# Cross-covariance attention then RWKV channel mix on one core: batch 0 with one kind of norm matmul, smaller last groups, and a block 0 in halves

## The chip, the cores and the metric

The kernel runs on one core of a Trainium2 chip. The metric is device time in microseconds (us). The engines have short names in the profile: PE (TensorE, matmul; PEld is its weight load), DVE (VectorE), ACT (ScalarE), POOL (GpSimd) and SP (SyncE, which only issues DMAs here).

## The reference

There are four batches of q, k and v, each 6208 x 256 in fp32. Per batch:

```python
qn = q / (np.linalg.norm(q, axis=1, keepdims=True) + 1e-06)
kn = k / (np.linalg.norm(k, axis=1, keepdims=True) + 1e-06)
s = kn.transpose(0, 2, 1) @ qn / tau
a = softmax(s)                      # over the last axis, 256 x 256
x = v @ a
# channel mix, with w_k 256x1024, w_v 1024x256, w_r 256x256
xk = mu_k * x + (1 - mu_k) * x_prev # x_prev: x one row earlier, 0 in the first row
xr = mu_r * x + (1 - mu_r) * x_prev
out = sigmoid(xr @ w_r) * (np.maximum(xk @ w_k, 0) ** 2 @ w_v)
```

The norms run over the 6208 rows, so nothing of a batch's output can begin before all of its q and k have been read.

## The kernel before, in words

**Two phases for batch 0, then one long pipeline.** q and k of batch 0 are loaded first, in fp32, by SP's queue. From its attention matrix a_sb the kernel then computes the output block by block: a block has 512 rows, there are 12 blocks per batch, 48 in all, and one block of leftover rows at the end. While the blocks run, q and k of the next batch are loaded (as bf16, by POOL's queue) and their products are slipped in between, in units of 128 rows.

**Batch 0, by groups.** `sizes` gives the groups: one of 64 rows (64 partitions, one row each), eleven of 512 rows (four rows per partition) and two of 256 rows (two per partition). `group_load` (L121) issues two DMAs, q and k, into fp32 buffers of which there are six each. `group_cast` (L138) makes a bf16 copy on DVE (L142) and squares on ACT (L144). `unit_matmul` (L171) adds k against q into S (s_ps, L182). The sums of squares come by one of two ways. Up to group `DIRECT` = 9, `group_norms` (L191) multiplies a ones matrix with the squares into the tile ssq_ps (L197), with one row in 32 lines of the array; from group 10 on, `norms_direct` (L203) uses the squares as weights and one column of ones as the moving operand, so that 128 sums land on 128 partitions of the tile `bank` (L210). Before group 10's matmuls ssq_ps is copied out by DVE (L225) and turned by four fp32 matmuls into the same `bank` (L232). `keep_warm(n)` (L509) issues n matmuls whose result is not used (junk_ps, L513); groups 5 to 9 have three each.

**From S to the first block.** `roots` takes the square root of the four columns in `bank` on ACT (L249), which needs a table load; `evac` copies S out of PSUM on ACT (L265); one activation on a tile `gate` loads the Exp table (L586). `invert` adds 1e-6 and takes the reciprocal on DVE (L257, L258) and makes two diagonal matrices rq_d (L260). `turn` (L272) multiplies S with these, which transposes and scales it into st_ps; `exp` (L280) takes exponentials and row sums on ACT; `weigh_dve` (L293, L294) divides. `v_transpose_pe` (L325) transposes a block of v on PE. `x_first` (L357) multiplies v with a_sb for block 0: one 512-column PSUM tile for each of the two d rows, the first copied out by ACT (L367), the second by DVE (L368). For later blocks `x_half` does this, one d row at a time (L352, L354).

**The pipeline.** The loop `for i in range(-2, NBLK - 1)` has eight steps j per i. Each step issues, in this order: `finish` (tanh on ACT, L469; product on DVE, L470; output DMA) of block i, one piece of a batch's softmax chain if one is due, `up(i + 1, j)` (two matmuls with w_k, L423, and a relu on ACT into kr, L428), `square` (kk = kr * kr on DVE, L441), `down(i, j - 1)` (with w_r, L456, and w_v, L460), `x_half`, `mix_delta` and `mix` of block i + 2 (DVE, L398 and L408), and in the steps named by `slots` one unit of the next batch: its two S matmuls, and ahead of it the squares of the next two rows on ACT (L163). The squares are added up on DVE by `next_add` (L169), at most once in steps 1, 6 and 7 of a block, and in step 2 at the end of a batch. The scheduling is manual: every engine runs its instructions in the order in which the program issues them. PSUM tiles rotate by tag; kT_ps, junk_ps and vT_ps share three buffers, x_first's tiles and vr_ps share two. `early` are the first four units of batch 1, whose matmuls are done at i = -1 and whose squares at i = 0. Block 1's v is transposed on PE before the loop and copied out by ACT; blocks 2 and 3 in the loop, copied out by DVE (L335); the others by a transposing DMA.

Of the kernel before, what the change touches and what calls it, by code (L numbers as in the profile page):

```python
# [10 lines left out]
F32 = mybir.dt.float32  # L11
# [7 lines left out]
def kernel(  # L19
# [44 lines left out]
    thirty2 = const.tile([P, P], F32, name="thirty2")  # L64
    nc.vector.memset(thirty2, 1.0 / 32)

# [26 lines left out]
    summed = set()  # L93
    DIRECT = NB - 3

    def sizes(b):
        return [1] + [S] * (NB - 1) + ([S // 2] * 2 if b == 0 else [S])
# [23 lines left out]
    def group_load(b, g):  # L121
# [3 lines left out]
        if b == 0:  # L125
            qk2 = pq.tile([P, S, 2, C], BF16, name="qk2", tag="qk2", bufs=4)
# [44 lines left out]
    def unit_matmul(b, g, s):  # L171
# [3 lines left out]
        if t0:  # L175

            cov[b] = (ps.tile([P, 2, C], F32, name="s_ps", tag="s_ps" if b else "vr_ps", bufs=1 if b else 2),
                      ps.tile([P, 2 * C], F32, name="ssq_ps", tag="vr_ps", bufs=2) if b == 0 else None)
        s_ps = cov[b][0] if b or g <= DIRECT else cov["s"]
# [5 lines left out]
        if s == n - 1 and b == 0:  # L185
            if g > DIRECT:
                norms_direct(g)
            else:
                group_norms(b, g)

    def group_norms(b, g):  # L191

        rows, n = rows_of(b, g)
        ssq_ps = cov[b][1]
        qk2 = groups[b, g][1]
        for u in range(n):
            nc.tensor.matmul(ssq_ps[32 * u:32 * (u + 1)], ones[:rows, :32],  # L197
                             qk2[:rows, u].rearrange("p i c -> p (i c)"),
                             start=u not in summed, stop=g == DIRECT, tile_position=(0, 32 * u),
                             skip_group_check=True)  # L200
            summed.add(u)

    def norms_direct(g):  # L203

        rows, n = rows_of(0, g)
        qk2 = groups[0, g][1]
        for u in range(n):
            flat = qk2[:rows, u].rearrange("p i c -> p (i c)")
            for i in range(4):
                nc.tensor.matmul(bank[0][:, C + i:C + i + 1], flat[:, i * P:(i + 1) * P], ones[:rows, 0:1],  # L210
                                 start=False, stop=g == len(sizes(0)) - 1 and u == n - 1, skip_group_check=True)

    def softmax_pieces(b):

        s_ps, ssq_ps = cov.pop(b) if b else cov[b]
# [7 lines left out]
        def copies():  # L223
            cov["ssq"] = pn.tile([P, 2 * C], F32, name="ssq", tag="ssq", bufs=1)
            nc.vector.tensor_copy(cov["ssq"], ssq_ps)  # L225

        def gather():

            cov["s"] = cov[b][0]
            bank[b] = ps.tile([P, 2 * C], F32, name="bank", tag="xT_ps", bufs=2)  # L230
            for i in range(4):
                nc.tensor.matmul(bank[b][:, C + i:C + i + 1], cov["ssq"][:, i * P:(i + 1) * P], thirty2[:, 0:1],  # L232
                                 start=i == 0, stop=False, skip_group_check=True)

# [5 lines left out]
        def norms():  # L240
            bank[b] = ps.tile([P, 2 * C], F32, name="bank", tag="xT_ps", bufs=2)
            for t, rows in ((sums.pop((b, "left"))[:, 0], L), (sums.pop(b), P)):
                for i in range(4):
                    nc.tensor.matmul(bank[b][:, C + i:C + i + 1], t[:rows, i * P:(i + 1) * P], ones[:rows, 0:1],
                                     start=rows == L and i == 0, stop=rows == P, skip_group_check=True)

        def roots():
            if b == 0:
                nc.scalar.activation(rn, bank[b][:, C:C + 4], AF.Sqrt)  # L249
            else:  # L250
                nc.scalar.copy(rn, bank[b][:, C:C + 4])
# [463 lines left out]
```

## Time and profile before

| | us |
|---|---|
| median of 8 runs | 514.49 |
| lowest and highest | 513.57, 515.03 |
| the profiled execution: its own time | 513.71 |
| the profiled execution: span, first to last instruction | 511.9 |
| mean granted TensorE clock | 0.996 |
| first fp32 load issued | 0.74 |
| last square of batch 0 ends (ACT, L144) | 36.74 |
| square root (ACT, L249) | 38.45 |
| first projection matmul of block 0 (PE, L423) | 45.67 |

How to read it: a line of the timeline has start, duration, engine, source line, operation, tile written from tiles read, the count of merged instructions, and in brackets the idle time before it with what ended it. A matmul's duration includes its way through the array, so matmuls overlap; the distance between two starts is what one costs. A line of the stretches has the stretch, its length, the busy time of PE, PEld, DVE, ACT and POOL (with counts), the granted clock as a share of full speed, the busy share of the DMA engines and GB/s.

### The profile page before, as it was taken

The page shows a single profiled execution, that of the slowest core. Times are in us where ns is not written, and L with a number is a line of the kernel's source. Part 1 is how long each engine was busy: PE and PEld are TensorE (multiplying, and loading weights), DVE is VectorE, ACT ScalarE, POOL GpSimd, SP SyncE. Part 2 cuts the span into 40 slices and gives each one's busy share as a digit, 9 for nine tenths or more (in the row PEclk, how much of TensorE's full clock was granted, in tenths as well). Part 3 has the DMA queues.
Part 4 walks back from the last instruction along what each step waited for, and adds up shares of the span by engine and source line. Part 5 has one row for each costly group of instructions (what it writes and reads, how often), then busy time and mean ns, then how long its engine had stood idle before and what let it go on. Part 6 is the DMA issues. An engine that isn't in the chain of part 4 may idle for free.

```text
span 511.9 us, 9496 instructions
## 1 busy us (share of the span) xinstructions
PE 494.2 (97%) x3540; PEld 336.4 (66%) x3540; DVE 439.8 (86%) x725; ACT 449.9 (88%) x924; POOL 99.8 (20%) x146
## 2 busy tenths in 40 slices
PE   3889999999999999999999999999999999999996
PEld 2454666766576667667666667667666666666675
DVE  4556899999999999999979999999878787878884
ACT  5886999999899999999899999999887888888784
POOL 0044342223054132221243133000131100000000
PEclk9989999999999999999999999999999999999999
DMA  8999999999999999998599999926496773423123
GB/s 314 410 312 198 197 167 183 140 176 199 215 177 188 174 193 161 193 193 132 99 152 208 163 198 178 182 71 119 83 181 132 123 126 90 100 81 85 44 81 103
DMA packets 133462, 83.46 MB, mean 163 GB/s; under 512 B 50660, under 2 KB 126760, under 8 KB 133416
## 3 DMA queue, kind: packets, MB, share of 16 engines
q0 software_dynamic: 56592, 33.01, 50.4%
q1 hardware_dynamic: 76656, 49.72, 43.9%
q8 instruction: 27, 0.44, 0.4%
q10 hardware_dynamic: 168, 0.13, 0.1%
q14 instruction: 19, 0.16, 0.1%
HBM read 78.71 MB, written 25.43 MB: 203 GB/s over the span
## 4 chain that ended last, share of the span: by engine, by line
PE 85%; DMA 5%; DVE 4%; ACT 4%; issue 1%; SPq 0%; DVEq 0%
PE vr_ps L460 31%; PE kT_ps L423 30%; PE vr_ps L456 8%; PE xT_ps L352 7%; PE s_ps L182 6%; DMA f<-in_k_dram 5%; ACT kr L428 1%; DVE acc L169 1%; DVE xk L408 1%; DVE kk L441 1%; PE st_ps L272 1%; ACT sq L163 1%; ACT xT L354 1%; DVE delta L398 1%; PE junk_ps L513 0%
## 5 line engine op out<-in xcount | busy, mean ns | idle before, releaser
L428 ACT ACTIVATE kr<-kT_ps 128x512 bf16<-128x512 f32 (+1 forms) x392 | 232.7, 605 | 28.9 <-PE kT_ps L423 24.9
L423 PE MATMUL kT_ps<-xk,w_k_sb 128*128 128x512 bf16 (+1 forms) x784 | 231.2, 377 | 0.4 <-DVE xk L408 0.2
L460 PE MATMUL vr_ps<-w_v_sb,kk 128*128 128x256 bf16 x1536 | 231.0, 273 | 0.1
L460 PEld LDWEIGHTS <-kk 128*128 128x128 bf16 x1536 | 149.6, 98 | 58.9 <-DVE kk L441 1.1
L470 DVE SCALAR_TENSOR_TENSOR res<-res,vr_ps 128x256 f32<-128x256 f32 x192 | 79.9, 416 | 44.1 <-ACT res L469 44.1
L441 DVE TENSOR_TENSOR kk<-kr 128x1536 bf16<-128x1536 bf16 (+2 forms) x148 | 116.9, 790 | 0.2 <-ACT kr L428 0.2
L423 PEld LDWEIGHTS <-w_k_sb 128*128 128x128 bf16 x784 | 75.8, 98 | 28.6 <-issue 1.2
L169 DVE TENSOR_TENSOR acc<-acc,sq 128x1024 f32<-128x1024 f32 x69 | 84.0, 1218 | 0.0
L182 PE MATMUL s_ps<-qk 128*128 128x256 bf16 x392 | 73.0, 287 | 5.9 <-DVE qk L142 5.9
L469 ACT ACTIVATE res<-vr_ps 128x256 f32<-128x256 f32 x192 | 76.2, 397 | 1.3 <-PE vr_ps L460 1.3
L456 PE MATMUL vr_ps<-w_r_sb,xr 128*128 128x256 bf16 x384 | 73.3, 272 | 1.2 <-DVE res L470 1.2
L408 DVE SCALAR_TENSOR_TENSOR xk<-delta,mu_t,xT 128x512 bf16<-128x512 bf16 x96 | 71.4, 745 | 0.0
L408 DVE SCALAR_TENSOR_TENSOR xr<-delta,mu_t,xT 128x512 bf16<-128x512 bf16 x96 | 71.4, 745 | 0.0
L456 PEld LDWEIGHTS <-xr 128*128 128x128 bf16 x384 | 37.6, 98 | 46.4 <-issue 2.5
L354 ACT CAST xT<-xT_ps 128x512 bf16<-128x512 f32 x94 | 55.3, 589 | 12.1 <-PE xT_ps L352 12.1
L352 PE MATMUL xT_ps<-vT,a_sb 128*128 128x512 bf16 x188 | 55.9, 379 | 0.2 <-DVE vT L335 0.2
L136 POOL DMA_DIRECT2D qk<-in_q_dram x39 | 26.3, 673 | 142.3 <-ACT kr L428 61.0
L165 ACT ACTIVATE sq<-qk 128x1024 f32<-128x1024 bf16 (+1 forms) x49 | 50.8, 1036 | 0.0
L182 PEld LDWEIGHTS <-qk 128*128 128x128 bf16 x392 | 39.1, 102 | 17.3 <-issue 7.9
L315 POOL DMA_DIRECT2D v_bf<-in_v_dram x48 | 37.3, 781 | 50.0 <-DMA vT<-v_bf 21.3
L398 DVE TENSOR_TENSOR delta<-xT 128x1024 bf16<-128x1024 bf16 x48 | 32.9, 686 | 1.9 <-ACT xT L354 1.8
L144 ACT ACTIVATE qk<-f 128x1024 bf16<-128x1024 f32 (+2 forms) x28 | 26.0, 947 | 7.9 <-DMA f<-in_q_dram 4.6
(82 smaller groups left out, 214.1 us busy)
## 6 DMA issues: line engine op xcount, KB each, us to landing
out_dram<-res SPq DMA_DIRECT2D x47, 512.0 KB, 5.0
v_bf<-in_v_dram POOLq DMA_DIRECT2D x48, 256.0 KB, 10.1
qk<-in_q_dram POOLq DMA_DIRECT2D x36, 256.0 KB, 9.2
qk<-in_k_dram POOLq DMA_DIRECT2D x36, 256.0 KB, 10.1
f<-in_q_dram SPq DMA_DIRECT2D x11, 512.0 KB, 8.7
f<-in_k_dram SPq DMA_DIRECT2D x11, 512.0 KB, 9.6
vT<-v_bf SPq DMA_TRANSPOSE x44, 9.7
f<-in_q_dram SPq DMA_DIRECT2D x2, 256.0 KB, 8.8
```

The source lines that it names most:

```text
L169: nc.vector.tensor_tensor(sums[b], sums[b], t, op=OP.add)
L182: nc.tensor.matmul(s_ps[:, ih, :], rows_at(qk, b, g, 0)[:rows, s, ih * P:(ih + 1) * P], rows_at(qk, b, g, 1)[:rows, s, :], start=t0 and ih ...
L352: nc.tensor.matmul(xT_ps, a_sb[:, b, ih, dh * P:(dh + 1) * P], vT[:, :, ih, :], start=ih == 0, stop=ih == 1)
L354: nc.scalar.copy(xT[:, dh, 1:], xT_ps)
L408: nc.vector.scalar_tensor_tensor(o[:, dh], st[i, "d"][:, dh], mu[:, dh:dh + 1], st[i, "x"][:, dh, :M], op0=OP.mult, op1=OP.add)
L423: nc.tensor.matmul(kT_ps[:, :m], w_k_sb[:, dh, fh * P:(fh + 1) * P], xk[:, dh, :m], start=dh == 0, stop=dh == 1)
L428: nc.scalar.activation(kr, kT_ps[:, :m], AF.Relu, scale=0.5 ** 0.5)
L441: nc.vector.tensor_tensor(st[i, "kk"][:, fh // 4 * 4 + lo:fh + 1, :m], kr, kr, op=OP.mult)
L456: nc.tensor.matmul(vr_ps[:, D:], xr[:, dh, s * P:(s + 1) * P], w_r_sb[:, dh, :], start=dh == 0, stop=dh == 1)
L460: nc.tensor.matmul(vr_ps[:, :D], kk[:, fh, s * P:(s + 1) * P], w_v_sb[:, fh, :], start=fh == 0, stop=fh == 7)
L469: nc.scalar.activation(res[:, s], vr_ps[:, D:], AF.Tanh, scale=0.5)
L470: nc.vector.scalar_tensor_tensor(res[:, s], res[:, s], 1.0, vr_ps[:, :D], op0=OP.add, op1=OP.mult)
```

## The change

- Batch 0's sums of squares are all made in the one-column way, into a `bank` of four columns that is opened at the start; ssq_ps, its copy and the gather are gone.
- The last 512 rows are split in groups of two, one and one rows per partition instead of two and two.
- `keep_warm` runs after every group from 5 on: three, then two, one and four matmuls.
- A first activation loads the square-root table at the start (the built program has two table loads instead of three: this one, and Exp's); the two small mu loads go from ACT's queue to POOL's.
- S is scaled by DVE while it is copied out of PSUM, and turned with the identity; ACT's copy and rq_d are gone for batch 0. The four turn matmuls run in the order of the scaled pieces.
- Block 0's v is transposed after the turn and copied out by DVE and ACT, a half each; the second half of a_sb is written in two pieces.
- Block 0 is computed in halves of 256 rows: x (both d rows of a half in one PSUM tile), the mix, and the first three of the eight `up` steps (`up_first`).
- Order: w_r and w_v are loaded ahead of block 2's v and batch 1's first group; `early` is gone, so batch 1's units begin at i = 0, j = 5, with seven per i from 1 to 6 and five at i = 7; block 1's v is transposed at (-1, 3), block 2's at (0, 3) and block 3's at (0, 6), all copied out by DVE; x, delta and xk of blocks 1 and 2 come at j = 4 to 7 instead of 0 to 5.

The marks @@ give the line before the change; `mix_tiles` only allocates delta, xk and xr.

```diff
...
-        return [1] + [S] * (NB - 1) + ([S // 2] * 2 if b == 0 else [S])
+        return [1] + [S] * (NB - 1) + ([2, 1, 1] if b == 0 else [S])
@@ L173
         if t0:
-            cov[b] = (ps.tile([P, 2, C], F32, name="s_ps", tag="s_ps" if b else "vr_ps", bufs=1 if b else 2),
-                      ps.tile([P, 2 * C], F32, name="ssq_ps", tag="vr_ps", bufs=2) if b == 0 else None)
-        s_ps = cov[b][0] if b or g <= DIRECT else cov["s"]
+            cov[b] = ps.tile([P, 2, C], F32, name="s_ps", tag="s_ps" if b else "vr_ps", bufs=1 if b else 2)
+            if b == 0:
+                bank[0] = ps.tile([P, 4], F32, name="bank", tag="xT_ps", bufs=2)
+        s_ps = cov[b]
         qk = groups[b, g][0]
...
         if s == n - 1 and b == 0:
-            if g > DIRECT:
-                norms_direct(g)
-            else:
-                group_norms(b, g)
...
+            for u in range(n):
+                flat = groups[0, g][1][:rows, u].rearrange("p i c -> p (i c)")
+                for i in range(4):
+                    nc.tensor.matmul(bank[0][:, i:i + 1], flat[:, i * P:(i + 1) * P], ones[:rows, 0:1],
+                                     start=g == 1 and u == 0 and i == 0, stop=te, skip_group_check=True)
...
-        s_ps, ssq_ps = cov.pop(b) if b else cov[b]
+        s_ps = cov.pop(b)
         rn = pn.tile([P, 4], F32, name="rn")
...
@@ L257
             for h in range(2):
-                nc.vector.tensor_scalar_mul(rq_d[:, h * P:(h + 1) * P], ident_f, rn[:, h:h + 1])
+                if b:
+                    nc.vector.tensor_scalar_mul(rq_d[:, h * P:(h + 1) * P], ident_f, rn[:, h:h + 1])
+                else:
+                    nc.vector.tensor_scalar_mul(s_sb[:, h], s_ps[:, h], rn[:, h:h + 1])
             if inv_tau != 1.0:
@@ L267
             st_ps[b] = ps.tile([P, 2, C], F32, name="st_ps", tag="xT_ps", bufs=2)
-            for ih in range(2):
-                for dh in range(2):
-                    nc.tensor.matmul(st_ps[b][:, ih, dh * P:(dh + 1) * P], s_sb[:, dh, ih * P:(ih + 1) * P],
-                                     rq_d[:, dh * P:(dh + 1) * P], start=True, stop=True)
+            for n in range(4):
+                ih, dh = (n % 2, n // 2) if b == 0 else (n // 2, n % 2)
+                nc.tensor.matmul(st_ps[b][:, ih, dh * P:(dh + 1) * P], s_sb[:, dh, ih * P:(ih + 1) * P],
+                                 rq_d[:, dh * P:(dh + 1) * P] if b else ident_f, start=True, stop=True)
@@ L288
-        def weigh_dve():
-            for ih in range(2):
-                nc.vector.reciprocal(sm[:, ih:ih + 1], sm[:, ih:ih + 1])
-                nc.vector.tensor_scalar_mul(a_sb[:, b, ih, :], e_sb[:, ih], sm[:, ih:ih + 1])
+        def weigh_dve(ih):
+            nc.vector.reciprocal(sm[:, ih:ih + 1], sm[:, ih:ih + 1])
+            for dh in (slice(0, C),) if ih == 0 else (slice(0, P), slice(P, C)):
+                nc.vector.tensor_scalar_mul(a_sb[:, b, ih, dh], e_sb[:, ih, dh], sm[:, ih:ih + 1])
         if b == 0:
-            return [copies, gather, roots, evac, invert, turn, exp, weigh_dve]
+            return [roots, invert, turn, exp, weigh_dve]
...
+        if evac is None:
+            return [lambda e=e, h=h: e(vT[:, h:h + 2], vT_ps[:, h:h + 2])
+                    for e, h in ((nc.vector.tensor_copy, 0), (nc.scalar.copy, 2))]
+        evac(vT, vT_ps)
@@ L357
         st[0, "x"] = xT
+        mix_tiles(0)
+        delta, xk = st[0, "d"], st[0, "xk"]
         nc.vector.memset(xT[:, :, 0:1], 0.0)
...
+        def go():
+            vT = st[0, "vT"]
+            x_ps = [ps.tile([P, 2, M // 2], F32, name="x_ps", tag="vr_ps", bufs=2) for a in range(2)]
+            for ih in range(2):
+                for a in range(2):
+                    for dh in range(2):
+                        nc.tensor.matmul(x_ps[a][:, dh], a_sb[:, 0, ih, dh * P:(dh + 1) * P],
+                                         vT[:, 2 * a:2 * a + 2, ih, :], start=ih == 0 and dh == 0, stop=ih == 1,
+                                         skip_group_check=True)
+            H = M // 2
+            nc.scalar.copy(xT[:, 0, 1:1 + H], x_ps[0][:, 0])
+            nc.vector.tensor_copy(xT[:, 1, 1:1 + H], x_ps[0][:, 1])
+            nc.scalar.copy(xT[:, :, 1 + H:], x_ps[1])
+            for a in range(2):
+                c = slice(a * H, (a + 1) * H)
+                nc.vector.tensor_tensor(delta[:, :, c], xT[:, :, a * H + 1:(a + 1) * H + 1], xT[:, :, c], op=OP.subtract)
+                for dh in range(2):
+                    nc.vector.scalar_tensor_tensor(xk[:, dh, c], delta[:, dh, c], mu_k_t[:, dh:dh + 1],
+                                                   xT[:, dh, c], op0=OP.mult, op1=OP.add)
+        return go
+    def up_first(fh, a):
+        H = M // 2
+        c = slice(a * H, (a + 1) * H)
+        if (fh, a) == (0, 0):
+            st[0, "kk"] = p2.tile([P, 8, M], BF16, name="kk", tag="kk", bufs=2)
+            st[0, "kr", 0] = p2.tile([P, 4, M], BF16, name="kr", tag="kr", bufs=2)
+        if a == 0:
+            st[0, "kT", fh] = ps.tile([P, M], F32, name="kT_ps", tag="kT_ps", bufs=3)
+        kT_ps = st[0, "kT", fh][:, c]
+        for dh in range(2):
+            nc.tensor.matmul(kT_ps, w_k_sb[:, dh, fh * P:(fh + 1) * P], st[0, "xk"][:, dh, c],
+                             start=dh == 0, stop=dh == 1)
+        nc.scalar.activation(st[0, "kr", 0][:, fh, c], kT_ps, AF.Relu, scale=0.5 ** 0.5)
@@ L503
-    nc.scalar.dma_start(mu_rows[0:2], moe_mu_k.rearrange("(h p) -> h p", p=P))
-    nc.scalar.dma_start(mu_rows[2:4], moe_mu_r.rearrange("(h p) -> h p", p=P))
+    nc.scalar.activation(gate, ones[:, 0:1], AF.Sqrt)
+    nc.gpsimd.dma_start(mu_rows[0:2], moe_mu_k.rearrange("(h p) -> h p", p=P))
+    nc.gpsimd.dma_start(mu_rows[2:4], moe_mu_r.rearrange("(h p) -> h p", p=P))
@@ L518
         group_cast(0, g)
-        if g == DIRECT + 1:
-            copies, gather, roots, evac, invert, turn, exp, weigh = softmax_pieces(0)
-            copies()
-            gather()
         for s in range(sizes(0)[g]):
             unit_matmul(0, g, s)
-        if 5 <= g <= DIRECT:
-            keep_warm(3)
+        if g >= 5:
+            keep_warm({S: 3, 2: 2, 1: 1}[sizes(0)[g]] if g < len(sizes(0)) - 1 else 4)
         if g == NB - 1:
@@ L575
     v_load(1)
+    nc.gpsimd.dma_start(w_r_sb, moe_w_r.rearrange("(ko ki) d -> ki ko d", ki=P))
+    nc.gpsimd.dma_start(w_v_sb, moe_w_v.rearrange("(fo fi) d -> fi fo d", fi=P))
+    v_load(2)
     next_load()
-    nc.gpsimd.dma_start(w_r_sb, moe_w_r.rearrange("(ko ki) d -> ki ko d", ki=P))
-    v_load(2)
-    nc.gpsimd.dma_start(w_v_sb, moe_w_v.rearrange("(fo fi) d -> fi fo d", fi=P))
     v_load(3)
     next_load()
+    x_go = x_first()
+    roots, invert, turn, exp, weigh = softmax_pieces(0)
     roots()
-    evac()
     nc.scalar.activation(gate, ones[:, 0:1], AF.Exp)
-    keep_warm(2)
-    go = v_transpose_pe(0, nc.vector.tensor_copy)
     invert()
-    keep_warm(2)
     turn()
-    go()
-    keep_warm(6)
+    vT_lo, vT_hi = v_transpose_pe(0, None)
     exp()
-    weigh()
-    x_first()
-    keep_warm(7)
-    v_transpose_pe(1, nc.scalar.copy)()
-    keep_warm(2)
-    early = units[:S]
-    pos["mm"] = pos["sq"] = S
+    vT_lo()
+    vT_hi()
+    weigh(0)
+    weigh(1)
+    keep_warm(3)
+    x_go()
+    keep_warm(4)
+    pos["mm"] = pos["sq"] = 0
@@ L621
                     piece()
-            if 0 <= i + 1 < NBLK:
+            if i == -1 and j < 3:
+                for fh, a in (((0, 0), (1, 0), (2, 0), (0, 1)), ((1, 1),), ((2, 1),))[j]:
+                    up_first(fh, a)
+            elif 0 <= i + 1 < NBLK:
                 up(i + 1, j)
@@ L632
                 down(i - 1, 7)
-            if i + 2 < NBLK:
+            if 0 < i + 2 < NBLK:
                 n = i + 2
-                full = 0 < n < NBLK - 1
-                if j in (0, 2) and full:
-                    x_half(n, int(j > 0))
-                if j == 3:
+                at = (4, 5, 6, 6, 7) if n < 3 else (0, 2, 3, 4, 5)
+                if n < NBLK - 1:
+                    for dh in range(2):
+                        if j == at[dh]:
+                            x_half(n, dh)
+                if j == at[2]:
                     mix_delta(n)
-                if j in (4, 5):
-                    mix(n, "xk", int(j > 4))
+                for dh in range(2):
+                    if j == at[3 + dh]:
+                        mix(n, "xk", dh)
...
                 mix(i + 1, "xr", int(j > 0))
-            if (i, j) in ((-1, 5), (0, 4)):
-                v_transpose_pe(i + 3, nc.vector.tensor_copy)()
+            if (i, j) in ((-1, 3), (0, 3), (0, 6)):
+                v_transpose_pe({(-1, 3): 1, (0, 3): 2, (0, 6): 3}[i, j], nc.vector.tensor_copy)
             if j == 5 and 4 <= i + 5 < NBLK - 1:
                 v_transpose(i + 5)
-            if i == -1 and j in (5, 6):
-                for u in early[:2] if j == 5 else early[2:]:
-                    unit_matmul(*u)
-            if (i, j) in ((0, 1), (0, 3)):
-                unit_square(*early[j - 1])
             elif i < 7:
-                slots = (1, 2, 3, 4, 5, 7) if i < 3 else (1, 2, 3, 4, 5, 6, 7)
+                slots = (1, 2, 3, 4, 5, 6, 7)
             elif i == 7:
-                slots = (1, 2, 7)
+                slots = (1, 2, 3, 4, 7)
```

## The prediction

> **What bounds the kernel now.** I read the page's first part, then the granted clock and busy times by stretch, then the timeline of the first 60 us, then TensorE's timeline alone.
>
> ```profile
> span 511.9 us, 9496 instructions
> PE 494.2 (97%) x3540; PEld 336.4 (66%) x3540; DVE 439.8 (86%) x725; ACT 449.9 (88%) x924; POOL 99.8 (20%) x146
> ```
>
> TensorE (PE) is the bound on average. Only the first 137 us can change, because the change touches batch 0, block 0 and the order of work in blocks 0 to 9. The stretches (us, busy us per engine, granted clock, DMA share, GB/s) split that part:
>
> ```profile
> 30.00:32.00 2.00, 0.71 (x3) 0.10 (x1) 1.51 (x3) 1.80 (x2) 0.00 (x0) 1.00 1.02 399
> 34.00:35.00 1.00, 1.00 (x20) 0.85 (x19) 0.83 (x3) 1.00 (x3) 1.00 (x2) 0.50 0.28 100
> 53.00:64.00 11.00, 10.88 (x80) 7.43 (x80) 9.03 (x16) 10.97 (x25) 3.26 (x6) 1.00 1.29 196
> 125.00:136.00 11.00, 9.82 (x69) 6.38 (x67) 11.00 (x17) 10.01 (x21) 0.15 (x1) 1.00 1.33 203
> ```
>
> Until 33 us the DMA is full (399 GB/s). At 34 us PE is the bound at half clock. From 53 to 64 ACT is full, at 125 DVE is full and PE waits. Next the serial path from the last load to the first projection:
>
> ```profile
> 36.76 1.28 ACT L249 ACT_TABLE_LOAD   x1
> 38.45 0.17 ACT L249 ACTIVATE rn<-bank 128x4 f32<-128x4 f32 x1 [0.41 <-PE bank L210]
> 39.76 1.13 PE L272 MATMUL st_ps<-rq_d,s_sb 128*128 128x128 f32 x8
> 43.24 0.69 DVE L368 CAST xT<-xT_ps 128x512 bf16<-128x512 f32 x1 [0.69 <-PE xT_ps L365]
> 44.77 1.42 DVE L408 SCALAR_TENSOR_TENSOR xk<-delta,mu_t,xT 128x512 bf16<-128x512 bf16 x2
> 46.24 0.38 PE L423 MATMUL kT_ps<-xk,w_k_sb 128*128 128x512 bf16 x1 [0.19 <-DVE xk L408]
> ```
>
> The square root waits for PE and not for its table, which came 0.41 us earlier. From the first kT matmul (45.67) PE's work is fixed, so the end is that start plus work plus stalls. A matmul of 512 columns takes 0.215 us from start to start (two from 47.74 to 48.17), one of 256 takes 0.109. Longer distances are stalls; the large ones are here:
>
> ```profile
> 53.12 0.59 PE L352 MATMUL xT_ps<-vT,a_sb 128*128 128x512 bf16 x2 [0.23 <-DVE vT L335]
> ...
> 131.74 0.38 PE L456 MATMUL vr_ps<-w_r_sb,xr 128*128 128x256 bf16 x2 [0.82 <-DVE res L470]
> ...
> 134.20 0.38 PE L456 MATMUL vr_ps<-w_r_sb,xr 128*128 128x256 bf16 x2 [0.35 <-DVE res L470]
> ```
>
> Start to start, from 45.67 to 140 us they are 1.4 (up to 53), 1.0 (53 to 87) and 1.8 (127 to 137), 4.2 us in all. After 140 PE hardly stops, and nothing there changes.
>
> **Loads and norms.** The ssq matmuls, their copy (0.68, L225) and the gather (0.92 of PE at 32.23) go. 16 one-column matmuls per group come: eight took 0.21 (37.43 to 37.64), so 0.42, against 0.33 for the four ssq matmuls (24.43 to 24.76): +0.1 per 2.56 us group, in PE's idle time. Casts and squares stay; the last two groups of one row give ACT four 256-column squares for two of 512 (0.31 apart by the 64x256 squares, 1.24 for 1.15), so ACT ends near 36.9 instead of 36.74. The one extra pair of DMAs moves the same bytes: nothing, up to 0.1. The mu loads go to POOL: an issue there takes 0.7 to 1.3 us (v_bf 1.34, w_k 0.74), so mu lands 2 to 4 us later and PE and DVE begin group 1 that much later; DVE needs 0.69 per cast and a cast comes every 1.28, so the lag is gone by 15 us: nothing. The first table load hides before the first load lands (4.30). On POOL's queue w_r and w_v (0.72 and 0.92 of issue) go ahead of block 2's v and of batch 1's first pair; a v load lands 10.1 us after its issue in the median, so all are there by 52, and v is first used at 56, batch 1 at 59, w_v at 53: nothing.
>
> Tail, at full clock: the last full group's k cast ends at 34.15. PE then does eight S matmuls (0.87), 16 norms (0.42), junk 3 (0.65), S 0.43, norms 0.21, junk 2 (0.43), S 0.22, norms 0.11, junk 0.21, S 0.22, norms 0.11 plus 0.15 of latency: 38.2, of which junk is 1.3. Now it is 38.41. Gain 0.2. At half clock until 37.2, as now, it would be 1.2 later.
>
> The row for the clock: after PE stood still for 1.53 us (30.71 to 32.23) and then did the slow gather, the clock is 0.50 from 33.83 for 3.41 us. [...]
>
> **From the root to the first projection.** Root 38.26 to 38.43. The Exp table (1.28) and the gate (0.21) are over at 39.9, before they are needed. DVE: add and reciprocal (0.17, 0.18) to 38.85, then S scaled in two 128x256 pieces. Nearest rows: 0.35 (a_sb, L294) and 0.42 (res, L470, out of PSUM); I take 0.37, 0.30 apart: 39.26 and 39.55. The turn needs only the first piece to begin: 39.32, four fp32 matmuls at 0.25 and latency: 40.45 (now 40.89). Exp waits for all four, as now: 40.49. V's transposes now stand behind the turn on PE (0.45), so DVE's half copy of vT (0.36) ends at 41.33 and delays the weights: second half of a_sb 42.27 (now 42.54). ACT's half copy ends 42.08. PE: eight 256-column matmuls, first half complete at 42.72.
>
> Copies: the halves put both d rows of one half in one PSUM bank, and the built program makes DVE's copy wait for ACT's. Now the two run side by side from two banks (43.03 and 43.24). The price is one ACT copy, 0.38 by the res row. [...]
>
> So ACT to 43.14, DVE to 43.55, delta half 0.37 to 43.94, xk halves 0.40 each, 0.33 apart: 44.37 and 44.70. First kT matmul 44.43 (now 45.67): **-1.24**. The second half of xk is ready at 45.43 and 45.76.
>
> **From there on.** Block 1's eight transposes move from the junk before 45.67 into PE's counted work: **+0.45**. The four early units move to the block steps i = 1, 2 and 7: no work added; batch 1's softmax pieces then come two steps later, with four steps to spare before block 12 needs them. Stalls:
> - Halves: PE waits for xk 0.22, 0.18, 0.22, and for the first kT buffer (six ACT halves, 0.26 apart) 0.13: 0.75.
> - vT of block 1 is now DVE's, behind block 0's xr: PE waits from 47.80 to 48.30: 0.5.
> - Stall c: block 1's x now comes at j = 4 and 5: x ends at 49.6, ACT's copy at 50.44, kk (0.61) and delta to 51.3, xk 52.09 and 52.76. PE is through with block 0 at 50.46, and nothing is left to do there (the early units and vT of block 2 filled it): 1.69 + 0.45. The lower bound is the present stall there, 0.7.
> - Stall d: block 2. At j = 5 the first unit puts four squares (4 x 0.52) on ACT ahead of kr 6 and tanh; DVE's res waits for the tanh, and the second xk half (0.66) is queued behind res. ACT: x copy 60.1, squares 62.1, kr, tanh 63.0, res 63.4, xk 64.1. PE is there at 62.5: 1.6. Lower bound 0, if the squares find ACT idle earlier.
> - Later: DVE gets at most three adds per block (10.05 us with 1.13 each) against PE's 10.2 with seven units. Now block 8 has four adds, which makes the 1.8 at 127 to 137. I take 0.6 for all after 64; bounds 0.2 and 1.0.
>
> Sum 5.6 against 4.2: **+1.4**. Total -1.24 + 0.45 + 1.4 = +0.6 on the profiled execution's 513.71 us (span 511.9 and 1.8 around it): **514.3 us**. The runs' median is 514.49, 0.8 above that execution; on the median the sum would be 515.1. I keep 514.3, because the half-clock stretch that the new junk covers is the one thing I see there that need not fall the same in each run; this is a choice.
>
> **Rivals.** Noise first: 0.2% (1.0 us) is about what a measurement tells from no change, so "same" is 513.46 to 515.52.
>
> Rival A, faster: the two block stalls are smaller because ACT has idle time before the squares (c 1.4, d 0.6, later 0.3, in all 3.55): -1.24 + 0.45 - 0.65 = -1.4, 512.3 us. For it: ACT is lighter than now in block 1 (six square instructions instead of nine). Against it: the order on ACT and DVE is fixed.
>
> Rival B, slower: the stall at 50.5 to 52.8 throws PE's clock. It is longer than the 1.53 us that did so at 30.71. Half clock for 3.41 us costs 1.7 of PE's work, all of it on the path: 516.0 us. [...]
>
> Rival C, the change does not do what it says: one-column matmuls do not keep the clock, the tail runs at half clock: +1.2, 515.5 us.
>
> **Chances.** Forecast 0.42, A 0.33, B 0.17, C 0.08. Faster 0.34 (A and an edge), slower 0.22 (B, half of C, an edge), same 0.44. The range goes from A's 512.2 to 516.2 just over B; the forecast's own is 513.4 to 515.5.
>
> **What would show it.** Root at about 38.3 and clock 1.00 through 34 to 38 (else C); first kT at 44.4; kT of block 1 at 52 with a PE gap of about 2 us before it, and again at 62 to 64 behind xk (no gaps: A); no gap at 130 to 135; a clock of 0.50 after 52 is B. I would be wrong most easily in the two block stalls.

## The result, and the profile after

The changed kernel takes 516.99 us in the median (516.53 to 520.23) against 514.03 for the kernel before in the same comparison: a ratio of 1.0062, 95% interval 1.0048 to 1.0075. It is slower by 3 us, and outside the predicted range. Of its twelve runs seven had a mean clock of 0.998 or more and took 516.5 to 517.3, and five, the profiled execution (518.14 us, 0.993) among them, had 0.988 to 0.995 and took 518.1 to 520.2.

The first part of the page after:

```profile
span 516.3 us, 9740 instructions
PE 494.7 (96%) x3654; PEld 340.9 (66%) x3654; DVE 440.7 (85%) x730; ACT 449.5 (87%) x929; POOL 100.9 (20%) x148
```

DVE and ACT have as much work as before; the span is longer by 4.4 us, because PE waits more and, for 3.41 us, runs at half clock. By stretch (us, busy us of PE, PEld, DVE, ACT, POOL, granted clock, DMA share, GB/s):

```profile
30.00:32.00 2.00, 1.74 (x27) 1.16 (x25) 0.99 (x2) 1.70 (x2) 0.00 (x0) 1.00 1.01 396
34.00:35.00 1.00, 0.85 (x8) 0.77 (x8) 0.79 (x3) 1.00 (x3) 1.00 (x2) 1.00 0.23 71
53.94:66.82 12.88, 11.52 (x79) 7.58 (x78) 8.08 (x14) 10.28 (x21) 1.80 (x3) 0.87 1.23 185
125.00:136.00 11.00, 11.00 (x81) 7.65 (x79) 11.00 (x18) 10.97 (x26) 2.73 (x4) 1.00 1.37 190
```

PE is busy at 30 us and the clock is 1.00 at 34, as was meant; no run tells the new junk's share in this from that of the gather, which is gone. PE's gap at 125 to 136 is gone. In its place stands block 1 (53.94 to 66.82, 12.88 us), where PE stands still and the clock is 0.87. Before, block 1 took 11.01 us:

```profile
52.93:63.94 11.01, 10.82 (x79) 7.37 (x79) 9.04 (x16) 10.98 (x24) 3.33 (x6) 1.00 1.29 196
```

The path from the root to the first projection:

```profile
38.17 0.17 ACT L211 ACTIVATE rn<-bank 128x4 f32<-128x4 f32 x1 [1.45 <-PE bank L184]
38.36 1.28 ACT L583 ACT_TABLE_LOAD   x1
38.86 0.88 DVE L225 TENSOR_SCALAR s_sb<-s_ps,rn 128x256 f32<-128x256 f32 x2
39.40 1.16 PE L237 MATMUL st_ps<-ident_f,s_sb 128*128 128x128 f32 x8 [0.39 <-DVE s_sb L225]
42.90 0.38 ACT L340 CAST xT<-x_ps 128x256 bf16<-128x256 f32 x1 [0.80 <-PE x_ps L336]
43.30 0.43 DVE L341 CAST xT<-x_ps 128x256 bf16<-128x256 f32 x1 [0.79 <-ACT xT L340]
44.23 0.88 DVE L347 SCALAR_TENSOR_TENSOR xk<-delta,mu_t,xT 128x256 bf16<-128x256 bf16 x2
44.86 0.90 PE L362 MATMUL kT_ps<-xk,w_k_sb 128*128 128x256 bf16 x5 [0.92 <-DVE xk L347]
```

The first projection starts 0.81 us earlier than before (45.67). Then PE's timeline shows where more than that is lost:

```profile
52.86 0.39 PE L422 MATMUL kT_ps<-xk,w_k_sb 128*128 128x512 bf16 x1 [1.57 <-DVE xk L407]
53.52 0.81 PE L422 MATMUL kT_ps<-xk,w_k_sb 128*128 128x512 bf16 x3 [0.27 <-DVE xk L407]
...
66.41 0.38 PE L422 MATMUL kT_ps<-xk,w_k_sb 128*128 128x512 bf16 x1 [1.36 <-DVE xk L407]
...
161.11 0.79 PE L318 MATMUL xT_ps<-vT,a_sb 128*128 128x512 bf16 x2 [0.29 <-ACT a_sb L254]
```

These are the prediction's stalls c (start to start, less the matmul: 1.73 and 0.44) and d (1.53), and one that it had ruled out: block 12's x waits for batch 1's attention matrix (0.45 and 0.18). After 170 us nothing differs.

### The profile page after: what moved, and what is told of

Same layout as the page of the kernel before. It is cut to its first block, busy times and chain, and to the rows that moved or that the text cites. A ratio compares the mean times of both kernels' runs of the same rounds, so it can differ in the third digit from the quotient of the medians.

```text
span 516.3 us, 9740 instructions
## 1 busy us (share of the span) xinstructions
PE 494.7 (96%) x3654; PEld 340.9 (66%) x3654; DVE 440.7 (85%) x730; ACT 449.5 (87%) x929; POOL 100.9 (20%) x148
## 4 chain that ended last, share of the span: by engine, by line
PE 80%; DVE 7%; DMA 6%; ACT 6%; issue 1%; SPq 1%; DVEq 0%
PE vr_ps L459 29%; PE kT_ps L422 28%; PE vr_ps L455 7%; PE xT_ps L318 7%; DMA f<-in_k_dram 6%; PE s_ps L177 5%; ACT kr L427 2%; DVE acc L164 2%; ACT sq L158 2%; DVE kk L440 1%; DVE xk L407 1%; PE st_ps L237 1%; SPq L126 1%; DVE res L469 1%; ACT xT L320 1%
## 5 line engine op out<-in xcount | busy, mean ns | idle before, releaser
L427 ACT ACTIVATE kr<-kT_ps 128x512 bf16<-128x512 f32 (+1 forms) x389 | 230.0, 603 | 30.7 <-PE kT_ps L422 26.4
L407 DVE SCALAR_TENSOR_TENSOR xk<-delta,mu_t,xT 128x512 bf16<-128x512 bf16 x94 | 70.0, 746 | 0.1
L139 ACT ACTIVATE qk<-f 128x1024 bf16<-128x1024 f32 (+3 forms) x30 | 25.8, 894 | 8.7 <-DMA f<-in_q_dram 5.5
```

The source lines that it names most:

```text
L407: nc.vector.scalar_tensor_tensor(o[:, dh], st[i, "d"][:, dh], mu[:, dh:dh + 1], st[i, "x"][:, dh, :M], op0=OP.mult, op1=OP.add)
L427: nc.scalar.activation(kr, kT_ps[:, :m], AF.Relu, scale=0.5 ** 0.5)
```

## The experiments

T1, the first theory: what is lost lies behind block 0's first projection, in the new order (x of blocks 1 and 2 two to four steps later, no early units). R1: it lies in the new start. R2: in the halves. The column "rest" is span minus the start of the first kT matmul in each run's profile, which leaves the loads' jitter out; the kernel before has 466.2, the changed one 471.4, of which 1.7 is half clock (an estimate: half of the 3.41 us at 0.50). The ratio is estimated from all runs and need not be the quotient of the two medians (e1).

| run | median | before, same chip | ratio, 95% interval | rest |
|---|---|---|---|---|
| e1 start only | 514.56 | 514.86 | 1.0009, 0.9986 to 1.0031 | 471.6 |
| e2 all but the start | 516.94 | 514.86 | 1.0057, 1.0036 to 1.0078 | 470.0 |
| e3 start, halves, old order | 514.45 | 514.86 | 0.9989, 0.9971 to 1.0007 | 468.2 |
| e4 junk in the stalls | 517.14 | 514.86 | 1.0045, 1.0028 to 1.0061 | 469.9 |
| e5 early units back | 516.38 | 514.13 | 1.0043, 1.0030 to 1.0057 | 469.8 |
| e6 old places of x | 514.34 | 514.13 | 1.0009, 0.9999 to 1.0019 | 467.3 |
| e7 xk ahead of res | 516.32 | 514.13 | 1.0044, 1.0029 to 1.0060 | 468.9 |
| e8 e3, no add at step 2 | 513.81 | 514.13 | 0.9995, 0.9983 to 1.0006 | 466.7 |
| e9 e3, slots earlier | 515.59 | 514.36 | 1.0033, 1.0014 to 1.0053 | 468.1 |
| e10 before, slots earlier | 515.99 | 514.36 | 1.0027, 1.0013 to 1.0041 | 467.7 |
| e11 four banks | 516.73 | 514.36 | 1.0056, 1.0035 to 1.0077 | 469.9 |
| e12 e9 and four banks | 515.90 | 514.36 | 1.0031, 1.0011 to 1.0051 | 468.2 |
| e13 three banks | 517.78 | 514.43 | 1.0070, 1.0049 to 1.0091 | 469.8 |
| e14 e3, add on POOL | 514.66 | 514.43 | 1.0002, 0.9989 to 1.0014 | 469.0 |
| e15 e13's banks, e14 | 515.57 | 514.43 | 1.0017, 1.0006 to 1.0029 | 467.3 |

In the profiles of e1 and e3 PE waited for transfers for which it doesn't wait in the other profiles (2.18 for qk and 2.26 for vT in e1, 2.19 for vT in e3); without these waits their rest is 467.1 and 466.0.

### Which part: e1, e2, e3

e1 takes the changed kernel up to a_sb and the kernel before from there on; e2 the reverse. e3 keeps start and halves and puts the order back:

```diff
     x_go()
-    keep_warm(4)
+    v_transpose_pe(1, nc.scalar.copy)
+    keep_warm(6)
-    pos["mm"] = pos["sq"] = 0
+    early = units[:S]
+    pos["mm"] = pos["sq"] = S
...
-                at = (4, 5, 6, 6, 7) if n < 3 else (0, 2, 3, 4, 5)
...
+                full = 0 < n < NBLK - 1
+                if j in (0, 2) and full:
+                    x_half(n, int(j > 0))
+                if j == 3:
                     mix_delta(n)
...
+                if j in (4, 5):
+                    mix(n, "xk", int(j > 4))
...
+            if i == -1 and j in (5, 6):
+                for u in early[:2] if j == 5 else early[2:]:
+                    unit_matmul(*u)
```

> The new start alone (norms, groups, table, scaling of S, V's copy in halves, the second half of a_sb in two pieces), and from a_sb on the program of before: block 0 whole, the early units, the old loads and slots. Theory T1 (the loss comes from the new order after block 0's first projection: block 1's and block 2's x two to four steps later, the early units gone): nothing is lost here, and little is won, because a_sb is complete at 42.51 us in the changed kernel and at 42.54 in the one before; 513.8 us, between 513.2 and 514.2, against 514.0 before. Rival R1 (the loss comes from the start: sixteen one-column matmuls per group, smaller instructions, two copies that follow each other): 515.5 or more.

> The other half of the change: the start of before up to a_sb, then block 0 in halves, the new loads, units, slots and places of x. T1: as slow as the whole change, 517.0 us (516.4 to 517.6), with PE's waits for xk of 1.5 us and more ahead of blocks 1 and 2. R1: 514.0 to 514.8, since the start is the old one.

> The new start and block 0 in halves, but the old order: block 1's v transposed ahead of the loop and copied by ACT, the early units, the old loads and slots, x of blocks 1 and 2 at steps 0 and 2. T1: the 0.81 us that the first projection comes earlier is kept less 0.5 to 0.8 of waits inside block 0's halves, and the stalls ahead of blocks 1 and 2 are those of before: 513.7 us (513.2 to 514.2). Rival R2 (the halves are what costs: PE's waits for half-sized copies, twice as many instructions on ACT and DVE, and block 1's x pushed back by them): 515.5 or more.

T1 holds, R1 and R2 fall. The start alone changes nothing that can be measured, the rest alone is as slow as the whole, and start and halves in the old order are level with the kernel before. (Both lie 0.25 to 0.36 us above their bounds, and the kernel before takes 514.86 on that chip, against the 514.0 assumed. The waits for transfers are part of it.)

### Which cause within the order: e5, e6

e5 puts the early units, slots and loads back and leaves x late; e6 is e3 with the changed kernel's units, slots and loads, so that only x's places and V's transposes (block 1's copied by ACT) are old. The order of the loads was not varied by itself.

> The changed kernel, but batch 1's first four units are multiplied while block 0 runs, as before the change, with the old slots and the old order of loads; x of blocks 1 and 2 stays late. Theory T2 (two causes add up: x of blocks 1 and 2 late gives 1.0 to 1.5 us at each of the two blocks; the missing early units leave the first of the two stalls unfilled and put 0.4 us more work into blocks 3 to 12): the wait ahead of block 1's projection falls from 2.2 to about 1.3, the one of 1.5 ahead of block 2 stays, the gap of 1.5 to 1.8 in block 8 is back and the wait of block 12 for its attention matrix (0.6) is gone; 515.8 us (515.2 to 516.4). Rival R3 (the units alone are the cause): 514.0 to 514.5. Rival R4 (x alone is): 516.6 to 517.0.

> The opposite: the changed kernel with x, delta and xk of blocks 1 and 2 and V's transposes at their old places, and no early units, with the new slots and loads. T2: no wait of 1.5 ahead of block 2, and ahead of block 1 the 0.7 of the old order plus the 0.87 us of matmuls that filled it; 514.0 us (513.4 to 514.8), 2.5 us and more under the whole change. R3: 516.5. R4: 513.5.

Both as T2 has it, in the main. PE's timeline of e6, and that of e5:

```profile
51.45 0.39 PE L422 MATMUL kT_ps<-xk,w_k_sb 128*128 128x512 bf16 x1 [0.46 <-DVE xk L407]
52.11 0.38 PE L422 MATMUL kT_ps<-xk,w_k_sb 128*128 128x512 bf16 x1 [0.27 <-DVE xk L407]
```

```profile
136.14 0.38 PE L455 MATMUL vr_ps<-w_r_sb,xr 128*128 128x256 bf16 x2 [0.82 <-DVE res L469]
138.60 0.38 PE L455 MATMUL vr_ps<-w_r_sb,xr 128*128 128x256 bf16 x2 [0.35 <-DVE res L469]
```

With x early the wait ahead of block 1 is 0.62 and 0.44 (T2 had 1.57 in all), and the one ahead of block 2 is not there; block 12 still waits for a_sb. With early units and late x, stall c shrinks from 2.17 to 1.30 us, d grows from 1.53 to 1.91, block 12 no longer waits, and the waits for res of the kernel before are back, 0.99 and 0.51. Two things follow. Late x, with V's transposes, costs about 2.5 us (changed kernel to e6, the medians of the runs with a mean clock of 0.998 or more: 516.8 and 514.3). And the vanished gap of block 8 and block 12's wait are one trade: units later, gap gone, chain late.

### What makes stall d: e7

ACT and DVE ahead of stall d in the changed kernel:

```profile
61.81 0.59 ACT L320 CAST xT<-xT_ps 128x512 bf16<-128x512 f32 x1
62.29 1.15 ACT L158 ACTIVATE acc<-qk 128x512 f32<-128x512 bf16 x2
63.16 0.75 DVE L407 SCALAR_TENSOR_TENSOR xk<-delta,mu_t,xT 128x512 bf16<-128x512 bf16 x1
63.34 1.14 ACT L158 ACTIVATE sq<-qk 128x512 f32<-128x512 bf16 x2
64.86 0.38 ACT L468 ACTIVATE res<-vr_ps 128x256 f32<-128x256 f32 x1
```

Four squares stand ahead of the tanh (64.86), res waits for the tanh, and xk's second half is behind res. e7 moves only that half:

```diff
-                at = (4, 5, 6, 6, 7) if n < 3 else (0, 2, 3, 4, 5)
+                at = (4, 5, 6, 6, 7 if n == 1 else 6) if n < 3 else (0, 2, 3, 4, 5)
```

> The changed kernel with one instruction moved: the second half of block 2's xk is issued at step 6 instead of step 7, so that it stands ahead of the product (res) that waits for ACT's tanh. If it is that queue that makes PE wait ahead of block 2's projection, the wait falls from 1.53 to between 0 and 0.6 and the time to 515.5 us (515.2 to 516.0). Rival: the wait is for ACT's copy of x behind the squares, whatever stands on DVE; the wait stays above 1.2 and the time within 0.3 us of the whole change (516.7 to 517.2).

Its timeline, DVE and PE:

```profile
61.94 1.42 DVE L407 SCALAR_TENSOR_TENSOR xk<-delta,mu_t,xT 128x512 bf16<-128x512 bf16 x2
...
63.80 0.38 PE L422 MATMUL kT_ps<-xk,w_k_sb 128*128 128x512 bf16 x1 [0.19 <-ACT kr L427]
```

The halves of xk now run back to back, and PE's wait is 0.35, for a kT buffer. The rest falls by 1.0 us (468.9 against 469.8 to 470.0 in e2, e4, e11 and e13). The median, 516.32, is above the expected 516.0: three of the six runs took 515.56 to 516.03, three 516.61 to 517.66, with no trace to show what was longer in these.

### The clock: e4

```diff
+                if j == 0 and i in (0, 1):
+                    keep_warm((7, 6)[i])
                 up(i + 1, j)
```

> The changed kernel with seven unused matmuls (1.5 us of PE) where PE waits for xk ahead of block 1's projection, and six ahead of block 2's. They lie in time in which PE stands. If the stall at 50.9 us is what throws the clock at 54.6, the runs of 518 us and more go: all runs between 516.4 and 517.3, median 516.7, and a profile without a clock of 0.50 after 50 us. If the clock is thrown by something else, the spread stays at 516.5 to 520 and the median at 517.0. If the stalls are not idle time of PE after all, the junk is added to the path: 518 or more.

All six runs lie between 516.47 and 517.39 with clocks of 0.999 and more, none at 518; the junk does not lengthen the rest (469.9, against 471.4 less the 1.7 of half clock). Six runs are few, but the profiles point the same way. Here is PE (us, busy us, clock, DMA share, GB/s) in the changed kernel, then in e2 and in e13 (a later run), whose stall c is the same 1.73 and 0.45:

```profile
51.23:54.64 3.41, 1.57 (x10) 1.00 1.33 198
54.64:58.05 3.41, 3.41 (x15) 0.50 1.34 202
```

```profile
49.22:52.63 3.41, 1.84 (x10) 1.00 1.23 208
52.63:56.05 3.42, 3.15 (x20) 1.00 1.43 195
```

```profile
50.78:54.19 3.41, 1.63 (x7) 1.00 1.22 201
54.19:57.61 3.42, 3.36 (x26) 1.00 1.43 197
```

In the profiles of the two kernels the clock changes only at a start plus whole multiples of 3.413 us (before: 33.83, 37.25 and, at the end, 511.70, from 16.77; changed: 23.92, 27.33, 54.64, 58.05 and, at the end, 515.44, from 17.09); that start is 12.36 in e7 and 19.97 in e1, and e14's half clock (0.51 from 135.36 to 138.77) is 3.41 us long as well. In the changed kernel both parts of the stall, but for the first 0.1 us, fell into one such window, and the next one was at half clock; in e2 the second part fell into the next window, and nothing happened. But in e13 all of the stall but its last 0.06 us fell into one window too, and nothing happened either. So the place of the stall in the grid seems to count, without a sharp rule: of the five profiles with this stall unfilled (the changed kernel, e2, e7, e11, e13) one shows rival B's half clock. And a run's mean clock doesn't tell where its half clock lay: the changed kernel's profile has another such stretch from 23.92 to 27.33, while batch 0 is loaded, and in the profiles of e5 and e7 (mean clock 0.997) it lies there alone (25.62 to 29.03 and 19.19 to 22.60).

### Block 8's gap, and the search for a faster version: e8, e9, e10, e14

All work on the waits for res in block 8 of the old order. e8 drops batch 1's addition at step 2, e14 gives it to POOL; e9 (on e3) and e10 (on the kernel before) move two units forward:

```diff
-            if adds and adds[0][0] <= now[0] and (j in (1, 6, 7) or j == 2 and adds[0][1] == holds[0] and chain):
+            if adds and adds[0][0] <= now[0] and (j in (1, 6, 7) or j == 2 and i > NB and adds[0][1] == holds[0] and chain):
```

```diff
-                next_add()
+                next_add(nc.gpsimd if j == 2 and i < NB else nc.vector)
```

```diff
-                slots = (1, 2, 3, 4, 5, 7) if i < 3 else (1, 2, 3, 4, 5, 6, 7)
+                slots = (1, 2, 3, 4, 5, 6, 7)
...
-                slots = (1, 2, 7)
+                slots = (1,)
```

> The new start and block 0 in halves with the old order of the pipeline, and one more edit: no addition of squares at step 2 of a block for batch 1, so that block 8 has three additions on DVE instead of four and the last one goes to the next free step. The kernel before has its attention matrix for block 12 ready 5 us before it is needed. If the fourth addition is what makes PE wait for res twice in block 8 (0.86 and 0.51 us), both waits go and nothing comes in their place: 1.2 us under the same kernel with the addition at step 2 (514.45 in the last runs, of which late transfers are a part): 513.0 us (512.3 to 513.6), faster than before. Rival: DVE is full there in any case, the additions only move, and the waits with them: 514.0 to 514.6.

> The new start and block 0 in halves with the old order and the early units, and the slots of the change for i = 1 and 2 (seven instead of six), with one left at i = 7: batch 1's last squares come earlier, so that their additions need no fourth place in block 8. Theory T5 (the waits for res in block 8, 0.86 and 0.51 us in the old order, come from the additions that are due late; spread earlier they vanish, as they did in the changed kernel, and with the early units block 12 need not wait for its attention matrix as it does there): 513.0 us (512.4 to 513.5). Rival: ACT is full in block 1 (10.97 of 11.00 us before the change), and two more squares there push PE back by what block 8 gains: 514.0 to 514.6.

> The kernel before with the slots of the last one (seven at i = 1 and 2, one at i = 7) and nothing else. T5: the gain does not need the new start, so 1.0 us under the kernel before: 513.1 us (512.6 to 513.6). Rival as there: 514.0 to 514.6.

> New start, halves and old order, with batch 1's addition of squares at step 2 of block 8 made by POOL instead of DVE. Theory T6 (the two waits for res in block 8, 0.86 and 0.51 us, are DVE's time for a fourth addition of 1.22 us, wherever on DVE it is put; moving it to later steps only moved the wait, 0.95 us at kk): on another engine it is gone; 1.2 us less than the same kernel, 513.1 us (512.4 to 513.5), provided POOL takes less than about 4 us and does not slow DVE. Rival: DVE's instructions beside POOL's addition get longer, or the fold waits for it; 513.8 to 514.6.

e8: its rival holds. The waits for res fall to 0.37 and 0.13, and one of 0.95 for kk comes at 137. (Its expectation gave the chain 5 us to spare; by the trace of before it is 2.5.) e9 and e10: T5 is wrong. Block 2 (from its first relu to that of block 3) takes 10.78 instead of 9.74, and block 8's waits grow to 1.21, 0.51 and 0.35 to 0.56: four additions still fall to block 8. e14: the addition left DVE, and DVE's delta beside it took longer:

```profile
129.63 2.73 POOL L164 TENSOR_TENSOR acc<-acc,sq 128x1024 f32<-128x1024 f32 x1 [10.89 <-ACT xT L320]
130.39 2.52 DVE L397 TENSOR_TENSOR delta<-xT 128x1024 bf16<-128x1024 bf16 x1
134.82 0.38 PE L455 MATMUL vr_ps<-w_r_sb,xr 128*128 128x256 bf16 x2 [2.04 <-DVE res L469]
```

delta, 0.68 us elsewhere, takes 2.52 and ends 0.55 after POOL's addition. So T6 was not put to the test. No version beats the kernel before by what can be measured; e1, e3, e6, e8 and e14 are level with it.

### The first projection: e11, e13, and the combinations e12, e15

e11 gives each d row of each half its own bank; e13 has two banks for the first half, one for the second, whose copy is issued after the first delta. The core of e13:

```diff
-            nc.scalar.copy(xT[:, 0, 1:1 + H], x_ps[0][:, 0])
-            nc.vector.tensor_copy(xT[:, 1, 1:1 + H], x_ps[0][:, 1])
-            nc.scalar.copy(xT[:, :, 1 + H:], x_ps[1])
+            nc.scalar.copy(xT[:, 0, 1:1 + H], x_lo[0])
+            nc.vector.tensor_copy(xT[:, 1, 1:1 + H], x_lo[1])
             for a in range(2):
+                if a == 1:
+                    nc.scalar.copy(xT[:, :, 1 + H:], x_hi)
```

> The changed kernel with each d row of each half of block 0's x in a PSUM bank of its own, four banks instead of two, so that DVE's copy of the first half runs beside ACT's instead of after it (now it starts at 43.30, where ACT's copy ends). If that wait is on the path of the first projection, the first kT matmul comes 0.4 us earlier after the square root (6.3 instead of 6.69 us), and the time falls by 0.4: 516.3 us against 516.7 for undisturbed runs of the whole change. Rival: block 0's later halves and block 1's x are behind other work, so the stall ahead of block 1 grows by what is won and the time stays within 0.1.

> The changed kernel, block 0's first half of x in two banks of its own (one per d row), the second half as before in one bank, and its copy issued after delta of the first half. With four banks the two copies ran side by side (0.16 us apart), but delta then began only after ACT's copy of the second half, 1.11 us after the first copy's start, against 0.87 in the changed kernel. If it is only that order of issue, delta begins 0.6 to 0.7 us after it, the first kT matmul comes 0.2 to 0.3 us earlier after the root (6.4 to 6.5 us instead of 6.69), and undisturbed runs take 516.4 us instead of 516.7. Rival: delta still begins at 0.87 or later, nothing changes.

> All that should help together: the new start, block 0 in halves with its own banks, the old order of x with early units, and the earlier slots. By the two theories 0.4 under the version without the banks: 512.6 us (512.0 to 513.2), 1.5 under the kernel before. If block 1's x sets the end of block 0 whatever comes first, it is within 0.1 of the version without the banks.

> Both edits together: halves with the banks of the one, the old order and POOL's addition of the other. By both theories 0.25 us less than the latter: 512.9 us (512.2 to 513.4), faster than the kernel before by 1.2. If neither holds, 514.

The chain of waits of e11 (start, us, what):

```profile
42.83 0.38 ACT xT L340
43.21 0.56 ACT xT L343 x2
43.77 0.18 issue
43.94 0.44 DVE delta L346
```

Both theories missed. The copies do run side by side (42.83 and 42.99), but delta begins 0.5 us after the last copy that it needs (DVE's, over at 43.41), so the first kT matmul is where it was: 6.78 us after the root, 6.69 in the changed kernel. e13 gives the same (delta 1.12 us after the first copy's start, 0.54 after its inputs), though its program has delta ahead of ACT's second copy. The profile names that copy as the releaser, but delta reads nothing that it writes. In e1 the same gap (0.53) stands ahead of a delta that begins 0.85 us after ACT's last copy of x. In all five profiles with this gap (e1, e11, e12, e13, e15) the trace has an EVENT_SEMAPHORE instruction on DVE (0.02 us long in the kernel before, at 43.97) ahead of delta, and delta begins 0.46 to 0.48 us after its end; the kernel before and e10 have that instruction too, and there it is 0.04. What holds delta stays open. e12 and e15 add nothing to e9 and e14.

## Why the prediction was wrong, step by step

**The start: right.** Root at 38.17 (38.26 predicted), clock 1.00 from 34 to 38, so rival C falls. The Exp table load is over before the exponentials, at 40.60 (40.49). The half clock from 23.92 to 27.33 was not foreseen; the root is not later than predicted.

**First projection, -1.24: mis-sized, -0.81.** The scaled pieces of S take 0.44 each (0.37 taken), the last a_sb ends at 42.52 and x's first half is complete 0.18 later than summed; delta takes 0.43 (0.37) and the two xk halves end 0.88 after their start (0.73). DVE's half-sized bf16 operations cost more than half: 0.48 for 256 columns against 0.75 for 512. The bank wait is there (43.30, 0.03 after ACT's copy), but the 0.4 that e11's expectation saw behind it was not won: with four banks the wait was gone, DVE's copy then ended 0.58 after ACT's began instead of 0.83, and delta waited for something else.

**Halves 0.75: 0.99. vT 0.5: 0.51. Stall c 1.69 + 0.45: 1.73 + 0.44. Stall d 1.6: 1.53.** These were right in place and cause, and in size but for 0.24 us in the halves; e5, e6 and e7 show the causes of c and d. Rival A, with smaller stalls, is refuted.

**Later 0.6, between 0.2 and 1.0: 2.4. This is the step that failed.** PE's waits from 74 to 162 us add up to 2.41 (0.63 for a_sb, 0.26 for res, three times 0.22 for kk, and nine of 0.05 to 0.13), against 3.16 after 59 us in the kernel before. The prediction took 2.2 as saved there; 0.75 were. The nine small waits alone, 0.86, are more than the 0.6 that it left for all; in the kernel before such waits make 1.2 of the 3.16. Two errors made the rest (the prediction let only the first 137 us change). First, it had the gap of block 8 go with nothing in its place, while DVE's work had only moved to blocks 9 to 11. Second, "four steps to spare" was miscounted. Here are the fold (the first DVE step of batch 1's chain, L237 before and L199 after) and a_sb, with block 12's x in the trace of before, then fold and a_sb in that of after:

```profile
136.80 0.68 DVE L237 TENSOR_TENSOR sq<-acc 128x512 bf16<-128x512 f32 x1
153.47 0.92 ACT L289 ACTIVATE a_sb<-e_sb,sm 128x256 bf16<-128x256 f32 x2
156.89 0.59 PE L352 MATMUL xT_ps<-vT,a_sb 128*128 128x512 bf16 x2
```

```profile
143.70 0.69 DVE L199 TENSOR_TENSOR sq<-acc 128x512 bf16<-128x512 f32 x1
160.56 0.90 ACT L254 ACTIVATE a_sb<-e_sb,sm 128x256 bf16<-128x256 f32 x2
```

Before, a_sb is complete at 154.40 and block 12's x begins at 156.89: 2.5 us, two steps. The fold begins 20.1 us ahead of that x. In the changed kernel it begins 17.0 us ahead of the time at which x would begin without its wait (161.11 less 0.45), and 3.1 us of delay against 2.5 to spare leave the 0.6 that PE waits.

**The count of before, 4.2: 4.55 by the same rule** up to 170 us (four small waits of 0.1 after 137 us were left out), which takes back 0.35.

The sum with these sizes: the prediction's +0.6, plus 0.43 (projection), 0.24 (halves), 1.8 (later), less 0.35, is +2.7: 516.4 us on 513.71. The profiled execution less its 1.7 us of half clock is 516.4 as well, and the runs with a mean clock of 0.998 or more took 516.5 to 517.3.

**Rival B: its half clock is seen, and it was no rival.** It comes on top: the profiled run has 0.50 from 54.64 to 58.05, 1.7 us. The other four runs with a mean clock below 0.998 took as long or longer (518.35 to 520.23), but only the profiled one shows where its half clock lay. Rival B set the stall's length against the 1.53 us that threw the clock before; the length alone doesn't decide. The kernel before has 1.5 us of stall for res between 130 and 135 at a clock of 1.00, but in two pieces, and a boundary of its grid (16.77 plus 34 times 3.413 is 132.81) lies between them. In the profiled execution 1.73 and 0.44 us were enough, with PE busy for 1.57 of the 3.41 us from 51.23; in e13 the same two waits, with 1.63 busy, were not. The forecast weighed the stall's length and not its place in the grid of 3.413 us that the profiles show.

## What to carry to other kernels

When a step is moved later by some slots, count what it has to spare from the trace of the kernel as it is, end of the producer to start of the consumer, and set the move against it: here 2.5 us to spare stood against a delay of 3.1. A gap that goes because work moved is saved only as far as the new place has idle time on the engine that made the gap. And a start that is earlier is worth nothing if the next blocks' inputs come later: 0.8 us were won ahead of block 0 and about 2.5 lost with the late x of blocks 1 and 2.

## What the runs showed of the hardware

- The half clocks lie on a grid of 3.413 us (54.64 to 58.05 in the changed kernel, 33.83 to 37.25 in the kernel before) whose phase differs by run. PE busy 1.57 us (the changed kernel) and 1.37 (e14) of such a window was followed by 0.50 and 0.51; 1.63 (e13), 1.84 (e2, e11) and 1.85 (e7) was not. But 1.41 in e1 was not either, and 1.88 in the kernel before (30.42 to 33.83, with the fp32 matmuls of the gather, 0.92 us of PE) was, so busy time as the profile counts it gives no sharp threshold. In e14 and e15 the same stall of 2.2 us threw the clock once, and once not, cut in two by the grid (busy 2.22 and 2.58).
- Beside a 128x1024 fp32 addition on POOL (2.73 us) a DVE subtraction of two SBUF operands took 2.52 us instead of 0.68 and ended 0.55 us after POOL's addition, while res, which reads PSUM, kept its 0.41 (e14, delta at 130.39, res at 130.06).
- In single profiles PE stood for a transfer for 2.2 us (2.18 for qk and 2.26 for vT in e1, 2.19 for vT in e3), about as much as what was to be measured.
